# Cached attention on one core: PE's program for 24 of 32 batches written as a loop, with fixed slots for K and V

## The chip, the cores and the metric

The kernel runs on one core of a Trainium2 chip. The metric is the device time of one execution in microseconds; for the kernel before it is the median of three runs. A profiled execution is taken beside them.

## The reference

32 batches, 4 query positions each, 32 query heads and 4 K/V heads (8 query heads share one), 2048 cached positions, head size 128, all in bf16. It projects the queries, attends over the whole cache without a mask, and projects the result:

```python
q = (x @ wq).reshape(B, Sq, Hq, Dh).transpose(0, 2, 1, 3)     # x: [32, 4, 1024]
k = jnp.repeat(k_cache, rep, axis=1)                          # [32, 4, 2048, 128], rep = 8
v = jnp.repeat(v_cache, rep, axis=1)
scores = jnp.einsum("bhqd,bhkd->bhqk", q, k) * (Dh ** -0.5)
p = softmax(scores, axis=-1)
o = jnp.einsum("bhqk,bhkd->bhqd", p, v)
out = o.transpose(0, 2, 1, 3).reshape(B, Sq, Hq * Dh) @ wo    # wo: [4096, 1024]
```

K and V of one batch are 2 MB each, 128 MB over the 32 batches; wq and wo are 8 MB each.

## The kernel before, in words

**Data.** Every large load brings 2 MB (128 partitions of 16 KB) into one of seven slots of SBUF. The list `stream` gives the order: four pieces of wq, K of batches 0 and 1, and then, step by step, K of batch i+2 and V of batch i-2, at the end four slots' worth of wo. Load n goes to slot n % 7 and waits until the reader of load n-7 is done. SP issues all of them in this order, one queue, each behind the one before (L167 to L191), so a load that waits holds back all behind it.

**Work per batch.** PE does four things, in the order that the lists given to `pe_run` write out:
- `kt_fill`: K comes with positions on the partitions; 64 transposes against `ident`, in eight fills of eight, turn it over into three PSUM banks used as a ring (L250). DVE (five fills, L388) and ACT (fills 0, 1 and 7, L390) copy each fill to `KT_sb`, which has room for two batches. This is done two batches ahead.
- `qk`: 16 matmuls (four heads by four chunks of 512) write the scores of all 128 rows to `ps_s` (L262). DVE takes the row maximum (L445), ACT the exponential (L504), and DVE transposes the probabilities in blocks of 32 (L451); POOL (three groups of heads, L408) and ACT (one, L406) place them on the diagonal blocks of `PD_sb`, which has room for two batches.
- `pv`: 64 accumulating matmuls in four quarters against V (L281), two batches behind `qk`. DVE scales the result and masks it (L462).
- `o_tr`: four matmuls with `pick` transpose it (L310), DVE files it in `oT_sb` (L457).

Batch i on PE is: `qk` of i, fills 0 to 2 of batch i+2, the first two quarters of `pv` of i-2, fills 3 and 4, the other two quarters, fills 5 to 7, and `o_tr` of i-2. Batches 29 to 31 are interleaved by hand (`DRAIN` = 29), and then 64 matmuls project with wo (L362).

**Order and waits.** `Program` holds a list of operations per engine, written out in full for all 32 batches. Each engine has one semaphore that counts its named operations, each slot has one for its loads; `emit` puts a wait ahead of an operation for each semaphore whose value it needs and hasn't yet waited for. So PE's program is straight: 5064 matmuls and as many weight loads, one after the other.

The functions that the change touches, and what calls them:

Of the kernel before, what the change touches and what calls it, by code (L numbers as in the profile page):

```python
# [13 lines left out]
class Program:  # L14

    ENGINES = ("pe", "dve", "act", "pool", "sp")

    def __init__(self):
        self.ops = {e: [] for e in self.ENGINES}
        self.count = {e: 0 for e in self.ENGINES}
        self.event = {}

    def op(self, eng, fn, waits=(), name=None):
        if name is not None:
            assert name not in self.event, name  # L30
            self.count[eng] += 1
            self.event[name] = (eng, self.count[eng])
        self.ops[eng].append((tuple(waits), fn, name))

    def load(self, eng, fn, name, sem, value, waits=()):
        assert name not in self.event, name
        self.event[name] = (sem, value)
        self.ops[eng].append((tuple(waits), lambda e: fn(e).then_inc(self.sems[sem], 16), None))

    def emit(self, eng, handle):  # L40
        seen = {}
        for waits, fn, name in self.ops[eng]:
            need = {}
            for w in waits:
                s, n = self.event[w]
                need[s] = max(need.get(s, 0), n)
            for s, n in need.items():
                if seen.get(s, 0) < n:
                    handle.wait_ge(self.sems[s], n)
                    seen[s] = n  # L50
            ins = fn(handle)
            if name is not None:
                ins.then_inc(self.sems[eng], 1)


def bass_standalone__gqa_block_cached__sampling_kernel(
# [11 lines left out]
    REP = Hq // Hkv  # L68
# [6 lines left out]
    scale = float(Dh) ** -0.5  # L75
    NSLOT = 7
    SLOT = 8192
    NRING = 3
# [23 lines left out]
    with ExitStack() as es:  # L102
        sb = lambda name, shape, dt: es.enter_context(nc.sbuf_tensor(name, shape, dt))
        slots = sb("slots", [128, NSLOT, SLOT], BF16)
        KT_sb = sb("KT_sb", [128, 2, G, Sk], BF16)
        QT_sb = sb("QT_sb", [128, B, Hq, Sq], BF16)
        oT_sb = sb("oT_sb", [128, WE, WO_BLOCKS, NT], BF16)
# [23 lines left out]
        ps_oT = ring_f32[3][:, 256:384]  # L131
        late_o = [ring_f32[1][:, 0:128], ring_f32[3][:, 0:128]]
        late_oT = ring_f32[2][:, 0:128]

# [6 lines left out]

        pr.sems = {e: es.enter_context(nc.semaphore(f"s_{e}")) for e in Program.ENGINES}
        for n in ["x", "out", "v2"] + [f"slot{i}" for i in range(NSLOT)] + [f"wo{i}" for i in range(sum(map(len, WO_CUTS)))]:
            pr.sems[n] = es.enter_context(nc.semaphore(f"s_{n}"))


        stream = [("wq", i) for i in range(WQ_LOADS)] + [("k", b) for b in range(AHEAD)]
# [5 lines left out]
        stream += [("wo", i) for i in range(WO_LOADS)]  # L153
        slot_of = {l: n % NSLOT for n, l in enumerate(stream)}

        def freed(l):
            kind, i = l
            return {"wq": ("qproj", i), "k": ("kt", i, FILLS - 1), "v": ("pv", i, QUARTERS - 1)}[kind]

# [10 lines left out]
        n_wo = 0  # L170
        for n, l in enumerate(stream):
            kind, i = l
            waits = [freed(stream[n - NSLOT])] if n >= NSLOT else []
            s, v = f"slot{n % NSLOT}", 16 * (n // NSLOT + 1)
            if kind == "wq":
                pr.load("sp", fetch(slot(l), wq_v[:, i, :]), l, s, v, waits)
            elif kind in "kv":
                src = (k_cache if kind == "k" else v_cache)[i].rearrange("g (p t) d -> (g p) (t d)", t=NJ)
                if l == ("v", B - 1):
                    half = SLOT // 2  # L180
                    pr.load("sp", fetch(slot(l)[:, 0:half], src[:, 0:half]), l, s, v, waits)
                    pr.load("sp", fetch(slot(l)[:, half:], src[:, half:]), ("v2", i), "v2", 16, waits)
                else:
                    pr.load("sp", fetch(slot(l), src), l, s, v, waits)
            else:
                for k in range(i * BPL, (i + 1) * BPL):
                    for e0, e1 in WO_CUTS[k]:
                        at = (k - i * BPL) * WE * D
                        part = slot(l)[:, at + e0 * D:at + e1 * D]
                        pr.load("sp", fetch(part, wo_v[k][:, e0 * D:e1 * D]), ("wo", k, e0), f"wo{n_wo}", 16, waits)  # L190
                        n_wo += 1  # L191
        pr.op("sp", lambda e: e.dma_start(out_flat[:, :], out_sb).then_inc(pr.sems["out"], 16), ["out0", "out1"])
        pr.op("sp", lambda e: e.wait_ge(pr.sems["out"], 16))


        jobs = [("kt", b, f) for b in range(B) for f in range(FILLS)]
        job_index = {j: n for n, j in enumerate(jobs)}

        def consumer(b, f):
            return "act" if f in ACT_FILLS and (b, f) != (B - 1, FILLS - 1) else "dve"  # L200

        def ring_waits(job):
            n = job_index[job]
            if n < NRING:
                return [("q_evac", n)]
            return [("evac",) + jobs[n - NRING]]


        def last_in(r):
            return [job for n, job in enumerate(jobs) if n % NRING == r][-1]  # L210

# [24 lines left out]
        for a in range(WQ_LOADS):  # L236
            for j in range(NB):
                last = a == WQ_LOADS - 1
                name = ("q", j) if last else (("qproj", a) if j == NB - 1 else None)
                pr.op("pe", lambda e, a=a, j=j: pe_qproj(e, a, j), [("wq", a), "xT_evac"], name)  # L240
        pr.event[("qproj", WQ_LOADS - 1)] = pr.event[("q", NB - 1)]

        def kt_fill(b, f):
            job = ("kt", b, f)
            dst = ring_bf16[job_index[job] % NRING]

            def fn(e):
                for q in range(JPF):
                    j = f * JPF + q
                    ins = e.transpose(  # L250
                        dst[:, q * 128:(q + 1) * 128],
                        slot(("k", b))[:, j * Dh:(j + 1) * Dh],
                        ident[:, :],
                    )
                return ins

            pr.op("pe", fn, [("k", b)] + ring_waits(job), job)

        def qk(i, c):
            def fn(e):  # L260
                for g in range(G):
                    ins = e.matmul(  # L262
                        ps_s[32 * g:32 * (g + 1), c * 512:(c + 1) * 512],
                        lhsT=QT_sb[:, i, REP * g:REP * (g + 1), :],
                        rhs=KT_sb[:, i % 2, g, c * 512:(c + 1) * 512],
                        start=True,
                        stop=True,
                        tile_position=(0, 32 * g),
                    )
                return ins  # L270

            w = [("evac", "kt", i, f) for f in range(2 * c, 2 * c + 2)]
            if c == 0:
                w += [("q_evac", j) for j in range(NB)] if i == 0 else [("exp", i - 1)]
            pr.op("pe", fn, w, ("qk", i, c))

        def pv(b, quarter):
# [11 lines left out]

            w = [("v", b)] + [("place", b, g) for g in range(G)]  # L290
            if b == B - 1 and quarter >= QUARTERS // 2:
# [3 lines left out]
            elif b <= DRAIN - 2:  # L295
                w += [("o", b - 1), ("ot", b - 1)]
            elif b == DRAIN - 1:
                w += [("evac",) + last_in(1)]
            else:
                w += [("o", b - 2), ("ot", DRAIN - 2)]  # L300
            pr.op("pe", fn, w, ("pv", b, quarter))

        def o_tr(b):
            w = [("o", b), "pick"]
            if b >= DRAIN - 1:
                w += [("ot", b - 1), ("evac",) + last_in(2)]

# [28 lines left out]

        for i in range(DRAIN):
            steps = [("qk", i, ()), ("kt", i + AHEAD, (0, 1, 2))]
            if i >= LAG:
# [5 lines left out]
            if i >= LAG:  # L345
                steps.append(("ot", i - LAG, ()))
            pe_run(steps)
        pe_run([
            ("qk", B - 3, ()), ("kt", B - 1, (0, 1, 2, 3, 4, 5)),
# [32 lines left out]
        def evac(b, f):  # L382
            job = ("kt", b, f)
            src = ring_bf16[job_index[job] % NRING].rearrange("p (q g r) -> p g q r", g=G, r=32)
            dst = KT_sb[:, b % 2, :, f * JPF * 32:(f + 1) * JPF * 32].rearrange("p g (q r) -> p g q r", r=32)
# [73 lines left out]
        def dve_o(b):  # L459
# [4 lines left out]
                [("pv", b, QUARTERS - 1), ("rinv", b), "mask"] + ([("otr", b - 1)] if b > 0 else []), ("o", b))  # L464

        for i in range(DRAIN):
            dve_max(i)
            dve_fills(i + AHEAD, range(0, 5))
            dve_turn(i)
            if i >= LAG:  # L470
                dve_o(i - LAG)
# [51 lines left out]
        pr.op("act", lambda e: e.activation(out_sb[:, 512:1024], ps_s[:, 512:1024], ACT.Copy), [("oproj", 1)], "out1")  # L523

        block = es.enter_context(nc.Block())

# [49 lines left out]
```

## Time and profile before

| | |
|---|---|
| median of 3 runs | 370.23 us (370.18 to 370.35) |
| profiled execution | 370.08 us, of which the span is 368.3 us |
| granted TensorE clock | 0.995 |
| DMA | 152.24 MB, mean 413 GB/s over the span, 11711 packets |
| PE | busy 85% of the span; from 95 to 310 us 187.36 of 215 us |
| DVE, ACT, POOL | busy 69%, 65%, 50% |
| DMA share of the chain that ended last | 66% |

How to read it: a row of the page's groups or of a timeline has the line of the kernel, the engine, the operation with what it writes and reads, and times; in square brackets stands how long the engine was idle before, and what ended that. A row of a queue gives packets, MB and the share of the 16 DMA engines' span that the packets took. Queue q1 carries the kernel's loads and stores, q8 and q14 carry instructions. Rows that begin with "GB/s" cut their stretch of time into 40 equal slices. Time from issue to landing includes the time that a load stands behind others.

### The profile page before, as it was taken

The numbers are of one execution on the slowest core, as the hardware profiler recorded it, in microseconds if no ns is written. First come the engines' busy times: TensorE is split into PE (matmuls) and PEld (weight loads), VectorE is DVE, ScalarE is ACT, GpSimd is POOL, SyncE is SP. The second block draws the span as 40 slices with busy tenths as digits, with TensorE's granted clock in tenths as the row PEclk, the third lists the DMA queues.
The fourth block names the chain that finished last, engine by engine and source line by source line (L and its number), as shares of the span: only waits on it lengthen the run. The fifth ranks groups of instructions, "written<-read, shape, count | busy, mean of one in ns | idle before, by whom it ended". The sixth has DMA issues, their size and how long they took to land.

```text
span 368.3 us, 11026 instructions
## 1 busy us (share of the span) xinstructions
PE 312.9 (85%) x5062; PEld 271.5 (74%) x5064; DVE 254.3 (69%) x366; ACT 239.1 (65%) x197; POOL 186.0 (50%) x99
## 2 busy tenths in 40 slices
PE   0997867999988888878899888799888888899896
PEld 0896647888877777767788778697777777787842
DVE  0015877888877777778777777497778885799600
ACT  1016678888877778875777777678777775758200
POOL 9600066666655566665555555466666653547000
PEclk9999999999999999999999999899999999999999
DMA  8999999999999999999999999999999999999983
GB/s 319 432 429 427 432 424 425 421 425 427 425 423 427 424 425 429 425 425 430 426 425 424 424 425 427 425 425 425 425 427 423 424 424 429 431 421 415 422 352 121
DMA packets 11711, 152.24 MB, mean 413 GB/s; under 512 B 1296, under 2 KB 1296, under 8 KB 1936
## 3 DMA queue, kind: packets, MB, share of 16 engines
q1 hardware_dynamic: 11520, 151.26, 97.1%
q8 instruction: 40, 0.66, 0.7%
q10 hardware_dynamic: 144, 0.26, 0.2%
q14 instruction: 7, 0.06, 0.0%
HBM read 151.26 MB, written 0.26 MB: 411 GB/s over the span
## 4 chain that ended last, share of the span: by engine, by line
DMA 66%; PE 21%; ACT 9%; DVE 2%; issue 1%; SPq 0%
DMA slots<-in_v_cache_dram 52%; PE ps_o L281 10%; DMA slots<-in_k_cache_dram 7%; DMA slots<-in_wo_dram 7%; ACT KT_sb L390 5%; PE ps_a L250 3%; PE ps_b L250 3%; ACT P_sb L504 2%; ACT PD_sb L406 2%; PE ps_c L250 2%; DVE PC_sb L451 1%; PE ps_s L262 1%; PE ps_b L281 1%; PE ps_s L362 1%; DVE mx L445 1%
## 5 line engine op out<-in xcount | busy, mean ns | idle before, releaser
L408 POOL COPY PD_sb<-PC_sb 32x2048 bf16<-32x2048 bf16 x91 | 171.5, 1885 | 153.3 <-DVE PC_sb L451 144.9
L281 PE MATMUL ps_o<-slots,PD_sb 128*128 128x128 bf16 x1920 | 118.6, 220 | 29.8 <-DMA slots<-in_v_cache_dram 29.1
L281 PEld LDWEIGHTS ps_o<-slots,PD_sb 128*128 128x128 bf16 x1920 | 110.0, 99 | 34.1 <-DMA slots<-in_v_cache_dram 32.9
L406 ACT ACTIVATE PD_sb<-PC_sb 32x2048 bf16<-32x2048 bf16 x32 | 61.0, 1907 | 69.2 <-DVE PC_sb L451 69.2
L504 ACT ACTIVATE P_sb<-ps_s,negmx 128x2048 bf16<-128x2048 f32 x32 | 81.9, 2560 | 5.0 <-DVE negmx L446 4.3
L445 DVE TENSOR_REDUCE mx<-ps_s 128x1 f32<-128x2048 f32 x32 | 73.3, 2289 | 4.0 <-PE ps_s L262 3.2
L250 PE MATMUL ps_a<-ident,slots 128*128 128x128 bf16 x688 | 52.7, 219 | 3.4 <-DMA slots<-in_k_cache_dram 1.2
L250 PE MATMUL ps_c<-ident,slots 128*128 128x128 bf16 x680 | 52.4, 220 | 3.4 <-ACT KT_sb L390 2.1
L250 PE MATMUL ps_b<-ident,slots 128*128 128x128 bf16 x680 | 52.1, 219 | 2.1 <-ACT KT_sb L390 2.0
L388 DVE COPY KT_sb<-ps_c 128x1024 bf16<-128x1024 bf16 x54 | 36.8, 681 | 22.6 <-PE ps_c L250 22.4
L388 DVE COPY KT_sb<-ps_a 128x1024 bf16<-128x1024 bf16 x54 | 36.8, 681 | 18.7 <-PE ps_a L250 18.7
L388 DVE COPY KT_sb<-ps_b 128x1024 bf16<-128x1024 bf16 x53 | 36.1, 682 | 18.4 <-PE ps_b L250 18.3
L250 PEld LDWEIGHTS ps_a<-ident,slots 128*128 128x128 bf16 x688 | 41.0, 98 | 9.7 <-issue 5.2
L250 PEld LDWEIGHTS ps_c<-ident,slots 128*128 128x128 bf16 x680 | 40.9, 98 | 9.6 <-issue 5.2
L250 PEld LDWEIGHTS ps_b<-ident,slots 128*128 128x128 bf16 x680 | 40.4, 98 | 8.2 <-issue 4.2
L451 DVE STREAM_TRANSPOSE PC_sb<-P_sb 128x1024 uint32<-128x1024 uint32 x32 | 39.2, 1226 | 0.0
L390 ACT ACTIVATE KT_sb<-ps_a 128x1024 bf16<-128x1024 bf16 x32 | 32.8, 1025 | 3.5 <-PE ps_a L250 3.3
L390 ACT ACTIVATE KT_sb<-ps_b 128x1024 bf16<-128x1024 bf16 x32 | 32.8, 1024 | 2.9 <-PE ps_b L250 2.6
L262 PE MATMUL ps_s<-KT_sb,QT_sb 128*32 128x512 bf16 x512 | 33.5, 382 | 0.8 <-ACT P_sb L504 0.8
L390 ACT ACTIVATE KT_sb<-ps_c 128x1024 bf16<-128x1024 bf16 x31 | 31.7, 1024 | 0.2
L462 DVE SCALAR_TENSOR_TENSOR o_sb<-ps_o,rinv,mask 128x512 bf16<-128x512 f32 x30 | 21.4, 713 | 1.5 <-PE ps_o L281 1.5
L262 PEld LDWEIGHTS ps_s<-KT_sb,QT_sb 128*32 128x32 bf16 x512 | 10.7, 96 | 9.1 <-ACT P_sb L504 1.1
(46 smaller groups left out, 147.1 us busy)
## 6 DMA issues: line engine op xcount, KB each, us to landing
slots<-in_k_cache_dram SPq DMA_DIRECT2D x32, 2048.0 KB, 27.9
slots<-in_v_cache_dram SPq DMA_DIRECT2D x31, 2048.0 KB, 23.4
slots<-in_wq_dram SPq DMA_DIRECT2D x4, 2048.0 KB, 14.5
slots<-in_wo_dram SPq DMA_DIRECT2D x7, 1024.0 KB, 25.0
slots<-in_v_cache_dram SPq DMA_DIRECT2D x2, 1024.0 KB, 21.9
slots<-in_wo_dram SPq DMA_DIRECT2D x1, 512.0 KB, 25.4
slots<-in_wo_dram SPq DMA_DIRECT2D x2, 256.0 KB, 22.9
P_sb<-in_x_dram ACTq DMA_DIRECT2D x1, 256.0 KB, 8.1
```

Source lines behind the costliest of these rows:

```text
L250: ins = e.transpose(dst[:, q * 128:(q + 1) * 128], slot(("k", b))[:, j * Dh:(j + 1) * Dh], ident[:, :],)
L262: ins = e.matmul(ps_s[32 * g:32 * (g + 1), c * 512:(c + 1) * 512], lhsT=QT_sb[:, i, REP * g:REP * (g + 1), :], rhs=KT_sb[:, i % 2, g, c * ...
L281: ins = e.matmul(o_bank(b), lhsT=PD_sb[:, b % 2, j // 2, :, j % 2], rhs=v[:, j * Dh:(j + 1) * Dh], start=(j == 0), stop=(j == NJ - 1),)
L362: ins = e.matmul(ps_s[:, c * 512:(c + 1) * 512], lhsT=oT_sb[:, r, k, :], rhs=w[:, k % BPL, r, c * 512:(c + 1) * 512], start=(k == 0 and r ...
L388: pr.op("dve", lambda e: e.tensor_copy(dst, src), w, ("evac",) + job)
L390: pr.op("act", lambda e: e.activation(dst, src, ACT.Copy), w, ("evac",) + job)
L406: pr.op("act", lambda e: e.activation(dst, src, ACT.Copy), w, ("place", b, g))
L408: pr.op(eng, lambda e: e.tensor_copy(dst, src), w, ("place", b, g))
L445: pr.op("dve", lambda e: e.tensor_reduce(mx[:, i:i + 1], ps_s[:, :], AX.X, ALU.max), [("qk", i, 3)], ("max", i))
L451: pr.op("dve", lambda e: e.transpose(PC_flat[i % 2].bitcast(U32), P_sb.bitcast(U32)), [("exp", i)] + [("place", i - 2, g) for g in range(G ...
L462: pr.op("dve", lambda e: e.scalar_tensor_tensor(out=o_sb[:, :, :], in0=src, scalar=rinv[:, b:b + 1], in1=keep, op0=ALU.mult, op1=ALU.mult) ...
L504: pr.op("act", lambda e: e.activation(P_sb.rearrange("p (a r e) -> p a e r", r=32, e=2), ps_s[:, :].rearrange("p (a e r) -> p a e r", r=32 ...
```

## The change

**A loop on PE.** For batches 5 to 28 PE's program holds the operations of four batches once and runs them six times. `pe_loop` compares the six rounds, operation by operation: each event waited for must be the next in a row of six. It gives each such event of another engine a semaphore of its own that counts turns (`loop0`, `loop1`, ...), and drops waits on events that were waited for earlier in the same turn. `emit` writes the loop with a register `turn` and a register `landed` that rises by 16 for the DMA semaphores. Other engines' programs stay straight. To make the four batches identical in every turn:

- K of batch b (from 7) goes to slot b % 4, V of batch b (3 to 28) to slot 4 + b % 2. Earlier and later loads have slots by a table; the seventh slot takes one wq piece and the V of batches 0 and 29. The order of the loads is unchanged; what each waits for follows from the slot's last holder. The fourth wq piece counts as read when the whole Q projection is done.
- Fill f of a batch uses ring bank f % 3 whatever the batch, so a batch's first fill follows fill 6 of the batch before in its bank, the second fill 7, the third fill 5. The banks of the last batches' outputs are moved to match.
- Queries: DVE copies the 128x128 queries of batch i to one of two places in `QC_sb` (`dve_qc`, after the transposition of batch i-2 and ahead of `dve_o`), and `qk` reads them there for batches 5 to 28.
- `qk` no longer names the copies of its own K, and `pv` and `o_tr` name fewer events, since PE has already waited for these or for later ones of the same engine.

The diff, cut to its core:

```diff
+    def pe_loop(self, first, body, times):
+        self.loop = (first, body, times)
...
+                if same[0] in self.event:
+                    sem = self.event[same[0]][0]
+                    assert [self.event[e] for e in same] == [(sem, 16 * (n + 1)) for n in range(times)], same
+                    kept.append((sem, 16))
+                else:
+                    sem = f"loop{sum(map(len, self.body_waits)) + len(kept)}"
...
+                    kept.append((sem, 1))
...
+    def emit(self, eng, handle):
+        ops = self.ops[eng]
+        if eng != "pe":
+            self.straight(ops, eng, handle)
+            return
+        first, body, times = self.loop
+        self.straight(ops[:first], eng, handle)
+        landed = handle.alloc_register("landed")
+        handle.reg_mov(landed, 16)
+        with handle.Fori(1, times + 1) as turn:
+            for op, kept in zip(ops[first:first + body], self.body_waits):
+                for sem, step in kept:
+                    handle.wait_ge(self.sems[sem], turn if step == 1 else landed)
+                self.step(op, eng, handle)
+            handle.reg_add(landed, landed, 16)
+        self.straight(ops[first + body * times:], eng, handle)
...
+    BODY = 4
+    FIRST = 5
...
-        slot_of = {l: n % NSLOT for n, l in enumerate(stream)}
+        slot_of = {("wq", 0): 4, ("wq", 1): 5, ("wq", 2): 6, ("wq", 3): 3}
+        slot_of.update({("k", 0): 0, ("k", 1): 1, ("k", 2): 2, ("k", 3): 3, ("k", 4): 5, ("k", 5): 1, ("k", 6): 2})
+        slot_of.update({("v", 0): 6, ("v", 1): 0, ("v", 2): 4})
+        for b in range(FIRST + AHEAD, B):
+            slot_of["k", b] = b % 4
+        for b in range(FIRST - LAG, DRAIN):
+            slot_of["v", b] = 4 + b % 2
+        slot_of.update({("v", B - 3): 6, ("v", B - 2): 0, ("v", B - 1): 1})
+        slot_of.update({("wo", 0): 2, ("wo", 1): 3, ("wo", 2): 5, ("wo", 3): 4})
...
-            waits = [freed(stream[n - NSLOT])] if n >= NSLOT else []
-            s, v = f"slot{n % NSLOT}", 16 * (n // NSLOT + 1)
+            waits = [freed(held[slot_of[l]])] if slot_of[l] in held else []
+            held[slot_of[l]] = l
...
+        def bank(f):
+            return f % NRING
...
+        LAST_IN = {0: 6, 1: 7, 2: 5}
...
+        def ring_waits(b, f):
+            if f >= NRING:
+                return [("evac", "kt", b, f - NRING)]
+            return [("evac", "kt", b - 1, LAST_IN[f]) if b > 0 else ("q_evac", f)]
...
-                        lhsT=QT_sb[:, i, REP * g:REP * (g + 1), :],
+                        lhsT=(QC_sb[:, i % 2] if FIRST <= i < DRAIN else QT_sb[:, i])[:, REP * g:REP * (g + 1), :],
...
+        def dve_qc(i):
+            pr.op("dve", lambda e: e.tensor_copy(QC_sb[:, i % 2], QT_sb[:, i]),
+                  [("q_evac", j) for j in range(NB)] + ([("qk", i - 2, 3)] if i - 2 >= FIRST else []), ("qc", i))
...
+        loop_times = (DRAIN - FIRST) // BODY
+        assert (DRAIN - FIRST) % BODY == 0
+        pr.pe_loop(loop_first, (len(pr.ops["pe"]) - loop_first) // loop_times, loop_times)
```

## The prediction

> **What bounds the kernel now.** I read the page first: busy shares, then the queues.
>
> ```profile
> span 368.3 us, 11026 instructions
> ...
> PE 312.9 (85%) x5062; PEld 271.5 (74%) x5064; DVE 254.3 (69%) x366; ACT 239.1 (65%) x197; POOL 186.0 (50%) x99
> ...
> q1 hardware_dynamic: 11520, 151.26, 97.1%
> q8 instruction: 40, 0.66, 0.7%
> ...
> slots<-in_k_cache_dram SPq DMA_DIRECT2D x32, 2048.0 KB, 27.9
> slots<-in_v_cache_dram SPq DMA_DIRECT2D x31, 2048.0 KB, 23.4
> ```
>
> No engine is full, but the 16 DMA engines are: queue q1, the data, fills 97.1% of their span. The second queue is PE's own program: 40 packets and 0.66 MB, and 0.66 MB over PE's 5062 + 5064 instructions is 65 bytes each, so a packet of 16 KB is some 256 instructions. A load takes 23 to 28 us from issue to landing though 2 MB at 427 GB/s need 4.9 us: four or five loads are always queued.
>
> Next I asked what PE waits for. In the waits of 90 to 320 us and in PE's timeline:
>
> ```profile
> PEld ps_o L281 <- DMA slots<-in_v_cache_dram: 32.9, 22, 2.9
> ```
>
> ```profile
> 293.59 1.96 PE L281 MATMUL ps_o<-slots,PD_sb 128*128 128x128 bf16 x32 [1.18 <-DMA slots<-in_v_cache_dram]
> ...
> 304.96 1.96 PE L281 MATMUL ps_o<-slots,PD_sb 128*128 128x128 bf16 x32 [2.76 <-DMA slots<-in_v_cache_dram]
> ...
> 314.75 1.46 PE L281 MATMUL ps_o<-slots,PD_sb 128*128 128x128 bf16 x23 [1.18 <-DMA slots<-in_v_cache_dram]
> ```
>
> Each batch's first PV block starts when its V lands. The step is 9.79 us as a rule (two loads of 4.89) but now and then 11.37, as from 293.59 to 304.96. I wanted the reason, so I took the sixteen completion marks that the trace keeps for each load, one per DMA engine. For the first load they lie at 8.3 to 8.6 us; for the last W_O piece at 356.1 to 364.0. The earliest marks come every 4.893 us all the way, so some engines keep the full rate to the end. The latest fall behind them in five steps: 1.7 us after 23 us, 3.3 after 91, 4.7 after 160, 6.3 after 228, 8.0 after 292. Within a step the engines follow singly, each some 8.6 us after the last, and that is the spacing of the 40 instruction packets. So PE's packets go to eight engines in turn; each puts its engine back 1.6 us (8.0/5), and a load is complete only when the latest engine is. On two of the other engines the rarer fetches of DVE and ACT add up to 3.1 and about 1 us. The end of the kernel shows the same in the DMA answer for 350 to 368 us:
>
> ```profile
> GB/s 382 437 364 455 419 455 391 446 401 396 423 373 378 291 300 214 278 209 259 209 209 228 209 178 178 218 232 164 182 114 0 0 0 0 0 0 0 332 250 0
> ```
>
> From 356 us the rate is half: eight engines are through, eight have up to 8 us to go. Then 4.3 us of projection, copy and store to 368.3, and 1.8 us outside the span make 370.08, 0.15 below the median 370.23. In one line: the end is 356.1 + lag of the latest engine (7.9) + 4.3 + 1.8. What the change does to that lag decides.
>
> **The loop: how often PE's program is fetched.** A batch is 64 transposes, 16 QK, 64 PV and 4 output matmuls: 148, with weight loads 296 instructions. The loop writes four batches once for six turns, so 20 x 296 = 5920 of 10126 instructions disappear; 4206 stay, 16.4 packets. A body is 4 x 296 = 1184, with its waits about 1210: 4.7 packets.
> - If the body stays in PE's instruction memory, there are 16 packets that matter (in the kernel before, the fortieth came at 361.9 us, when its engine was nearly through). Over eight engines that is 2 each: lag 2 x 1.6 = 3.2, which is also what DVE's fetches leave on theirs, so no gain below that. 356.1 + 3.2 + 4.3 + 1.8 = 365.4. If a seventeenth falls before the end, 4.8 and 367.0.
> - If each turn fetches its body again, a turn costs 5 or 6 packets (a body of 4.7 that begins inside a block touches 5 or 6, and one is fetched ahead beyond the end). 11 outside the loop plus 36 to 40 make 47 to 51: 6 or 7 per engine, lag 9.6 to 11.2, total 371.8 to 373.4. If a block always goes to the same engine, one gets 7 or 8: up to 12.8 and 375.0.
>
> No row of this trace shows a jump back, so these two are the bounds, on both sides of zero. I take the first: the body is a small program, and eight engines taking turns for PE (DVE's three fetches all hit one engine) looks to me like eight places of 256 instructions, room for 4.7 blocks and one ahead. That is a weak reason, and I keep both ends.
>
> [...]
>
> **The jump itself.** If the target has to be fetched, PE stands still for it five times. Bounds: one packet, 1.07 us in the trace's packet records, to the 8.1 us that x takes from issue to landing; I take 3, a packet on top of the output's 2.0 us issue to landing. It hides in PE's waits for V: 1.2 us per batch, 4.7 per turn, and nothing after the last jump (about 275 us) is late by the end. Without that cover 5 x 3 = 15 us. If the target is there, a jump is nothing visible.
>
> **K in four slots, V in two.** Now a load waits for the load seven before it. After, V of batch b+2 waits for PV of batch b:
>
> ```profile
> 264.23 1.96 PE L281 MATMUL ps_o<-slots,PD_sb 128*128 128x128 bf16 x32 [1.19 <-DMA slots<-in_v_cache_dram]
> ...
> 266.92 1.95 PE L281 MATMUL ps_o<-slots,PD_sb 128*128 128x128 bf16 x32
> ```
>
> V lands at 264.2, its last PV ends at 268.9, so the next V is issued 4.9 us after the landing and the K behind it on SP at once (K's own slot came free four batches before). At that moment three loads, K, V and K, were ahead of it: 14.7 us. Margin for the latest engine: 14.7 - 4.9 - 2.0 (issue to landing of the small output store) = 7.8 us; an early engine has that less its lead, and where it runs dry it only loses lead. Towards the end, V of batch 28 has two loads ahead: margin 2.9. So nothing at the end moves, unless PE is later than that; then the excess is paid in full. V's issue to landing should fall to about 15 us, K's to 19. At the start K of batch 3 waits for the whole Q projection (28.5 us instead of 17.4), but K0 to K2 are in the queue until 37.7: nothing.
>
> **Waits, ring, copies.** The ring's first fill of a batch now waits for fill 6 of the batch before, its second for fill 7, which ACT copied out at 253.15 where PE began that fill at 252.47: 0.7 us later, with 0.6 to 1.2 us of waiting for V behind it; uncovered 24 x 0.7 = 17. Register waits: PE has 71 separate wait instructions of 51 ns now; five more per batch are 0.25 us, in the same cover. The 24 query copies on DVE: between 0.15 (128x1, L446) and 0.28 us (128x128 from PSUM, L457) each, after the transpose and ahead of the output scaling, for which PE's L310 waits; 24 x 0.28 = 6.7 us if uncovered, but DVE is 69% busy and PE's next wait is V. All zero in my sum; together they use most of a batch's 1.2 us, which is why the fourth case below has a chance.
>
> **The cases.** Smallest difference a measurement of this kernel can tell: about 0.2%, 0.7 us.
> 1. Body stays, 50%: 365.5, from 364.9 to 367.2. For it: the body is 4.7 blocks. Against: no row shows a block used twice.
> 2. Slower, body fetched every turn, 41%: 373.2, from 371.6 to 375.0. The place is the six turns' packets on PE's eight DMA engines; the price is 1.6 us for each packet above five on the latest engine. It decides from the point where PE keeps fewer blocks than the five or six of the body and the one ahead. The row that speaks for it is the 40 packets for 39.6 blocks, one new block at every crossing, which is what a memory without room for old blocks would show too.
> 3. No difference, 5%: 370.2. The loop runs, but the lag has another cause or the fetches stay as many and fall elsewhere. Against: steps and packets share spacing and count.
> 4. PE becomes the bound, 4%: stall, waits and ring use more than 4.7 us per turn. With a stall of 8.1 the excess is 3.4 in each of five jumps, on top of case 2: about 390.
>
> So faster 0.50, within 0.2% 0.05, slower 0.45. The predicted time is case 1's. The range reaches over case 2 to 374.0; left out are case 4, the upper fifth of case 2 and a little of case 1, about 0.15.
>
> **What would show it.** Right: the instruction queue q8 at 16 to 18 packets; none while the loop runs after its first turn; the sixteen marks of the last load within 3 to 5 us; PV steps of 9.8 us without one of 11.4; half rate at the end for 3 us instead of 8. Wrong: q8 at 45 or more, marks 10 us apart, an idle of PE above 1 us each fourth batch that ends in "issue"; then case 2. If V's issue to landing falls below 10 us or the DMA row shows gaps before 350 us, my margin for two V slots was wrong.

## The result and the profile after

The loop takes 365.65 us (365.61 to 365.71, four runs) against 370.21 us of the kernel before in the same session: ratio 0.9876, 95% interval 0.9859 to 0.9894. The forecast was 365.5. The profiled execution took 365.71 us, 363.9 of them the span, at a granted clock of 0.995.

From the page of the kernel after (busy time per engine; queues with packets, MB and share; loads with count, size and median time from issue to landing):

```profile
span 363.9 us, 11144 instructions
...
PE 313.3 (86%) x5062; PEld 271.5 (75%) x5064; DVE 256.2 (70%) x390; ACT 239.9 (66%) x197; POOL 186.0 (51%) x99
...
q1 hardware_dynamic: 11520, 151.26, 98.2%
q8 instruction: 16, 0.26, 0.3%
...
slots<-in_k_cache_dram SPq DMA_DIRECT2D x32, 2048.0 KB, 19.4
slots<-in_v_cache_dram SPq DMA_DIRECT2D x31, 2048.0 KB, 14.9
```

PE executes as many matmuls and weight loads as before, and q1 moves the same 151.26 MB. What has shrunk is q8: 16 packets instead of 40. In the trace's DMA records twelve of them lie between 21.0 and 118.4 us, four between 321.0 and 344.7, and none in the 203 us between, in which the second to sixth turns of the loop run (the first jump back is at 120.3 us, the sixth turn ends at 316.0).

What PE waits for from 90 to 320 us (engine, what it was about to do, what ended the wait: us in total, times, longest):

```profile
PEld ps_o L351 <- DMA slots<-in_v_cache_dram: 18.9, 21, 0.9
...
PE ps_b L317 <- ACT KT_sb L465: 6.8, 19, 0.4
...
PE ps_s L329 <- issue: 1.1, 5, 0.3
```

The first row had a longest wait of 2.9 us; it is 0.9 now. The other two rows are the two new costs on PE: the ring's second fill (6.8/19 = 0.36 us) and the five jumps back (1.1/5 = 0.22 us). In PE's timeline, a jump and two first PV blocks (start, time, what, idle time before it and its end):

```profile
120.84 1.05 PE L329 MATMUL ps_s<-KT_sb,QC_sb 128*32 128x512 bf16 x16 [0.25 <-issue]
...
300.49 1.96 PE L351 MATMUL ps_o<-slots,PD_sb 128*128 128x128 bf16 x32 [0.73 <-DMA slots<-in_v_cache_dram]
...
310.27 1.96 PE L351 MATMUL ps_o<-slots,PD_sb 128*128 128x128 bf16 x32 [0.72 <-DMA slots<-in_v_cache_dram]
```

The step is 310.27 - 300.49 = 9.78 us; in this stretch the kernel before had one of 11.37. At the end, the DMA rate from 350 to 364 us in 40 slices of 0.35 us:

```profile
GB/s 445 421 398 398 445 374 445 468 421 421 363 398 433 392 415 421 410 380 258 269 257 199 228 234 211 94 0 0 0 0 0 0 0 0 0 310 386 53 0 0
```

The reduced rate lasts from about 356.3 to 359.1, 2.8 us; in the row of the kernel before it lasts from about 356.3 to 363.5, 7.2 us. The sixteen completion marks of the last load lie at 356.75 to 359.53, where they were at 356.1 to 364.0. So the last piece of data is complete 4.47 us earlier, and the time falls by 4.56.

### The profile page after: what moved, and what is told of

The parts are those of the page before. It is cut to its first block, busy times and chain, and to the rows that moved or that the text cites. A ratio compares the mean times of both kernels' runs of the same rounds, so it can differ in the third digit from the quotient of the medians.

```text
span 363.9 us, 11144 instructions
## 1 busy us (share of the span) xinstructions
PE 313.3 (86%) x5062; PEld 271.5 (75%) x5064; DVE 256.2 (70%) x390; ACT 239.9 (66%) x197; POOL 186.0 (51%) x99
## 3 DMA queue, kind: packets, MB, share of 16 engines
q1 hardware_dynamic: 11520, 151.26, 98.2%
HBM read 151.26 MB, written 0.26 MB: 416 GB/s over the span
## 4 chain that ended last, share of the span: by engine, by line
DMA 59%; PE 29%; ACT 6%; DVE 3%; issue 1%; SPq 0%
DMA slots<-in_v_cache_dram 45%; PE ps_o L351 17%; DMA slots<-in_k_cache_dram 7%; DMA slots<-in_wo_dram 7%; PE ps_b L317 4%; ACT KT_sb L465 4%; PE ps_a L317 3%; PE ps_s L329 2%; PE ps_c L317 1%; DVE KT_sb L463 1%; ACT PD_sb L481 1%; PE ps_c L351 1%; PE ps_s L437 1%; DVE PC_sb L526 1%; ACT P_sb L585 1%
## 5 line engine op out<-in xcount | busy, mean ns | idle before, releaser
L463 DVE COPY KT_sb<-ps_a 128x1024 bf16<-128x1024 bf16 x64 | 43.8, 685 | 48.8 <-PE ps_a L317 48.7
L317 PE MATMUL ps_b<-ident,slots 128*128 128x128 bf16 x768 | 59.8, 221 | 11.6 <-ACT KT_sb L465 11.2
L465 ACT ACTIVATE KT_sb<-ps_b 128x1024 bf16<-128x1024 bf16 x63 | 64.6, 1025 | 5.1 <-PE ps_b L317 4.4
L317 PE MATMUL ps_a<-ident,slots 128*128 128x128 bf16 x768 | 59.1, 220 | 5.4 <-DVE KT_sb L463 3.6
L317 PEld LDWEIGHTS ps_a<-ident,slots 128*128 128x128 bf16 x768 | 45.9, 98 | 19.2 <-issue 15.8
L463 DVE COPY KT_sb<-ps_c 128x1024 bf16<-128x1024 bf16 x64 | 43.5, 680 | 6.1 <-PE ps_c L317 6.1
L317 PE MATMUL ps_c<-ident,slots 128*128 128x128 bf16 x512 | 39.6, 221 | 0.0
L317 PEld LDWEIGHTS ps_c<-ident,slots 128*128 128x128 bf16 x512 | 31.7, 99 | 0.2 <-DVE KT_sb L463 0.2
L329 PE MATMUL ps_s<-KT_sb,QC_sb 128*32 128x512 bf16 x384 | 25.1, 381 | 1.1 <-issue 1.1
L463 DVE COPY KT_sb<-ps_b 128x1024 bf16<-128x1024 bf16 x33 | 22.5, 681 | 0.6 <-PE ps_b L317 0.6
L437 PE MATMUL ps_s<-slots,oT_sb 128*128 128x512 bf16 x62 | 13.9, 379 | 1.0 <-DVE oT_sb L532 0.6
## 6 DMA issues: line engine op xcount, KB each, us to landing
slots<-in_k_cache_dram SPq DMA_DIRECT2D x32, 2048.0 KB, 19.4
slots<-in_v_cache_dram SPq DMA_DIRECT2D x31, 2048.0 KB, 14.9
```

What stands on the lines that cost most here:

```text
L317: ins = e.transpose(dst[:, q * 128:(q + 1) * 128], slot(("k", b))[:, j * Dh:(j + 1) * Dh], ident[:, :],)
L329: ins = e.matmul(ps_s[32 * g:32 * (g + 1), c * 512:(c + 1) * 512], lhsT=(QC_sb[:, i % 2] if FIRST <= i < DRAIN else QT_sb[:, i])[:, REP * ...
L437: ins = e.matmul(ps_s[:, c * 512:(c + 1) * 512], lhsT=oT_sb[:, r, k, :], rhs=w[:, k % BPL, r, c * 512:(c + 1) * 512], start=(k == 0 and r ...
L463: pr.op("dve", lambda e: e.tensor_copy(dst, src), w, ("evac",) + job)
L465: pr.op("act", lambda e: e.activation(dst, src, ACT.Copy), w, ("evac",) + job)
```

## The experiments

A "mark" is one of the sixteen completions that the trace keeps per load, one per DMA engine; "last mark" is the latest of the last W_O piece. Neither a mark nor a packet says which engine it belongs to: that is inferred from how the marks of a load lie. Times are medians, or single executions where the table says so, with the ratio to the kernel before on the same chip; on the chips of these runs that kernel took 370.10 to 370.25. The runs together:

| kernel | PE's packets | last mark, us | time, us | ratio (95%) |
|---|---|---|---|---|
| before | 40 | 364.0 | 370.21 | |
| after | 16 | 359.53 | 365.65 | 0.9876 (0.9859 to 0.9894) |
| e1: PE's program straight | 40 | 363.96 | 370.33 | 1.0002 (0.9993 to 1.0012) |
| e3: loop for half the batches | 30 | 362.46 | 368.78 | 0.996 (0.9945 to 0.9974) |
| e4: 20 rows of 16 KB | 16 | 375.06 | 381.47 | 1.0305 (1.0288 to 1.0322) |
| e5: the same rows in two loads | 16 | 364.47 | 370.64 | 1.0016 (1.0006 to 1.0025) |
| e10: the same bytes in one even load | 16 | 360.49 | 366.55 | 0.9906 (0.989 to 0.9923) |
| e6: body of 5.95 blocks | 18 | 379.70 | 387.16 | one execution |
| e7: body of 6.95 blocks | 64 | 466.21 | 473.87 | one execution |
| e2: body of eight batches | 43 | 366.67 | 372.46 | 1.0051 (1.0035 to 1.0068) |
| e8: the same with a hint | 42 | 365.46 | 373.49 | 1.0092 (1.0061 to 1.0123) |
| e11: V of batch 28 in the seventh slot | 16 | 359.59 | 365.72 | 0.9879 (0.9863 to 0.9896) |

The theory: PE's packets put eight DMA engines back, one at a time, and the kernel ends with the latest engine ("lag"). Rivals: the gain comes from what was rearranged for the loop, that is slots, ring, query copies and waits ("schedule"); or from the 0.39 MB that is no longer moved ("bytes").

**e1: everything but the loop.** Slots, ring banks, query copies and events are those of the kernel after; PE's program is written out.

```diff
-        if eng != "pe":
+        if True:
             self.straight(ops, eng, handle)
             return
```

> The changed kernel with PE's program written out straight again; slots, ring banks, query copies and the semaphores are the changed kernel's. Lag theory (the end is set by the DMA engine that PE's instruction packets put back most, 1.6 us each, eight engines in turn): 40 packets on q8, last load's marks 7 to 8 us apart or less only because early engines run dry, 370.2 us within 0.7. Schedule theory (fixed slots, ring banks and copies brought the gain): 365.7 with 40 packets. Bytes theory (0.4 MB less to fetch, shared by all 16 engines, 24 x 1.07 / 16 = 1.6 us): 367.3.

Measured 370.33 us. From its page, and from its DMA answer for 350 to 368 us (slices of 0.45 us):

```profile
span 368.6 us, 11124 instructions
...
q8 instruction: 40, 0.66, 0.7%
```

```profile
GB/s 400 455 419 401 455 382 400 437 437 401 473 400 401 437 401 419 382 419 437 419 382 446 373 382 410 364 246 209 200 118 0 0 0 0 0 0 0 100 378 105
```

With 40 packets the whole gain is gone, so the schedule theory falls. The rate row has a surprise: the long half-rate stretch is absent. The marks of the last load are only 1.9 us apart (362.05 to 363.96), yet the last one is where it was. With two slots for V the early engines had run dry at V of batch 28 (first mark at 327.3 where the full rate gives about 321.4) and lost their lead. The spread at the end is therefore no safe sign of the lag; the last mark is.

**e3: half the loop.** Batches 5 to 16 straight, 17 to 28 as three turns.

```diff
     FIRST = 5
+    LOOP_FIRST = 17
...
-        loop_times = (DRAIN - FIRST) // BODY
+        loop_times = (DRAIN - LOOP_FIRST) // BODY
```

> The loop only for batches 17 to 28 (three turns), batches 5 to 16 straight; everything else as changed. Lag theory: 16 + 12 x 303 / 256 = 30 packets, 3 or 4 per engine, lag 6.0 to 6.4, so 2.8 to 3.6 above 365.65: 368.4 to 369.3. Bytes theory: 14 packets x 1.07 / 16 = 0.9 above: 366.6. Schedule theory: 365.7.

Measured 368.78 us. Its page:

```profile
q8 instruction: 30, 0.49, 0.5%
```

Thirty packets over eight engines are at most four on one: 356.1 + 4 x 1.6 = 362.5, and the last mark is at 362.46. Lag theory met; bytes and schedule, which wanted 366.6 and 365.7, not.

**e4: delay without instructions.** To see whether a packet delays only its own engine, 20 rows of 16 KB, each a load to one partition and each in one packet, are put behind V of batches 5 to 24, into the free seventh slot. 327,680 bytes in all. V of batch 29, the next in that slot, waits for the last row, which landed at 306.3 us, before that load's turn came.

```diff
+            if l == ("v", B - 3):
+                waits.append(("row", LAST_ROW))
...
+                if kind == "v" and 5 <= i < 25:
+                    r = i - 5
+                    dst_row = slots[r:r + 1, 6, :]
+                    src_row = src[r:r + 1, :]
+                    pr.load("sp", fetch(dst_row, src_row), ("row", r), "row", 16 * (r + 1), [("pv", 0, QUARTERS - 1)])
```

> The changed kernel with 20 extra rows of K, 16 KB each and one packet each, loaded by SP behind the V of batches 5 to 24 into the seventh slot and never read: 0.33 MB, about what the loop saves in instruction bytes. Lag theory: if all rows go to one engine, it falls behind by 20 x 0.61 = 12.2 us on top of its own 0 to 3; the last marks stand 9 to 13 us later: 375 to 378. Bytes theory: 0.33 MB at 427 GB/s = 0.8 us: 366.4.

Measured 381.47 us, beyond the forecast. The rows left one completion each, where a load of 2 MB leaves sixteen (q1 has 11560 packets instead of 11520: twenty of 16 KB and twenty completions), so each ran on one engine, and by the marks it was the same for all: in the load whose first mark is at 199.23 us fifteen marks lie within 3.4 us, the sixteenth 8.6 behind the first. The last mark moved from 359.53 to 375.06, 0.78 us per row. I had taken 0.61, which is 16 KB at one engine's sixteenth of 427 GB/s. In the middle of the run a batch took 10.86 us by its last marks (235.3, 246.1, 256.9, 267.9) instead of 9.79, so 1.07 per row. The first rows only used up that engine's lead: the last marks are those of the kernel after until 153.6 us and fall behind from the next load on. At 1.07 each, 14 to 15 of the twenty rows make the 15.53 us, an estimate. The kind of effect is shown, the size of one row's delay was forecast too low. From 200 to 320 us (busy time with counts for PE, PEld, DVE, ACT, POOL; then clock, DMA share, rate):

```profile
200.00:320.00 120.00, 101.82 (x1650) 90.64 (x1648) 85.60 (x136) 81.30 (x66) 62.21 (x33) 0.96 0.97 399
```

Here one late engine held back all: V's slot comes free only when its latest part has been used, so the others ran dry, and the rate fell from the 428 GB/s of the kernel after (95 to 310 us) to 399.

**e5: the same rows in two loads.** Rows 0 to 15 beside V of batch 5, 16 to 19 beside V of batch 15.

```diff
+                if kind == "v" and i in (5, 15):
+                    r = i - 5
+                    lo, hi = ((0, 16), (16, 20))[r // 10]
+                    dst_row = slots[lo:hi, 6, :]
+                    src_row = src[lo:hi, :]
+                    pr.load("sp", fetch(dst_row, src_row), ("row", r), "row", 16 * (r // 10 + 1), [("pv", 0, QUARTERS - 1)])
```

> The same 20 extra rows of 16 KB as in the run with twenty single rows, but in two loads, 16 rows beside the V of batch 5 and 4 beside that of batch 15; never read. Lag theory: a load of 16 rows puts one on each engine, so every engine falls back by 0.6 to 1.1 us once and four engines twice: 0.6 to 2.1 above 365.65, 366.3 to 367.8. If the cost of the single rows was that of issuing many loads and not of the one engine, it falls in proportion, to 2/20 of 15.8 us: 367.2. Bytes theory: 366.4.

A miss: 370.64 us. The load of 16 rows did spread over the engines, but the marks show every engine 3.0 us late after it, and the small load took another 0.4 to 1. A further 0.95 of the 4.94 us at the last mark appears at 276.0 us, in the first load after a packet of q14 (272.1); no run follows that up. The rate from 98 to 112 us (slices of 0.35 us):

```profile
GB/s 468 374 421 328 515 468 421 468 375 281 187 281 94 234 421 234 281 187 140 140 140 375 234 515 234 304 468 281 421 421 421 421 515 421 375 375 468 468 375 421
```

For about 6 us, from 101 to 107, it lies mostly at 94 to 304. The 262 KB to 16 partitions put every engine back by 3.0 us, where 2 MB to all 128 take 4.9. No run here varied the partitions alone, so the reason for the 3.0 us is not shown, and e5 could not separate bytes from places.

**e10: the same bytes, evenly.** One load of 2560 bytes to each of 128 partitions, 327,680 bytes, beside V of batch 5.

```diff
+                if kind == "v" and 5 <= i < 6:
+                    r = i - 5
+                    dst_row = slots[:, 6, 0:1280]
+                    src_row = src[:, 0:1280]
+                    pr.load("sp", fetch(dst_row, src_row), ("row", r), "row", 16 * (r + 1), [("pv", 0, QUARTERS - 1)])
```

> The 0.33 MB of the twenty single rows once more, never read, now as one load over all 128 partitions (2560 bytes each) beside the V of batch 5, so that it is shared by engines and partitions as the kernel's own loads are. Lag theory: each of the 16 engines falls back by 20 KB at 27 GB/s = 0.8 us, none more than the others: 366.4. If the 15.8 us of the single rows, or the 5.0 of the two loads, came from the bytes or from the loads as such, it costs 5 or more: 370.6.

Measured 366.55 us, 0.90 above the kernel after; 0.33 MB at 427 GB/s are 0.77. The same bytes cost 0.9 us in one load on all engines and 15.8 in twenty loads on one. PE's 24 missing packets are 0.39 MB, 0.92 us if spread evenly; the change gained 4.56. So the number of bytes is not the cause, their place is.

**e6 and e7: how much PE keeps.** The fills of batches 7 to 30, those in the loop, repeat 5 or 9 of their transposes (the first result is overwritten by the same values). The forecasts put the body at about 1550 and 1806 instructions; the trace's records of one turn count 1523 and 1779, which is 5.95 and 6.95 blocks of 256 (1203, or 4.7, in the kernel after). PE becomes the bound (in e6 busy for 160.00 of the 160 us from 140 to 300), so here packets and idle times decide, not the total. The diff is that of e6; e7 has `range(9)`.

```diff
-                for q in range(JPF):
+                again = range(5) if FIRST + AHEAD <= b < DRAIN + AHEAD else ()
+                for q in [r % JPF for r in again] + list(range(JPF)):
```

> The changed kernel with 5 transposes in each fill of the loop written twice (same result), so that the body is 320 instructions longer, about 1550 or 6.1 blocks of 256. Only the packets of the instruction queue are read; PE becomes the bound by 40 x 0.056 us a batch and the time rises to 390 or more. If PE keeps eight blocks (7 or 8 with the one ahead): 17 or 18 packets. If it keeps fewer than seven: about 16 + 5 x 7 = 50. If the loop's blocks are kept whatever their number up to nine: 18.

> As the run before with 9 transposes more per fill: 576 instructions longer, about 1806 or 7.1 blocks, which touch eight and one ahead is a ninth. Only the packets are read; the time rises past 410. If PE keeps eight blocks: the turns fetch again, 16 + 5 x 8 or more = 50 to 60 packets; if it keeps nine or more: 19.

The packets of e6, then those of e7, each from its page:

```profile
q8 instruction: 18, 0.29, 0.3%
```

```profile
q8 instruction: 64, 1.05, 0.9%
```

And e7's waits from 60 to 330 us:

```profile
PE ps_s L330 <- issue: 26.0, 4, 6.6
```

5.95 blocks are kept, with no packet between 128.7 and 348.9 us; 6.95 blocks are fetched again in each turn, and each jump in this window leaves PE idle for about 6.5 us. The 64 packets are more than the 50 to 60 of the forecast: 45 above the 19 of a kept body, nine for each of the five jumps. The limit lies between the two bodies; where between them, no run shows. e6's time, 387.16 us, is a little under the 390 of its forecast. e7 is 86.7 us slower than e6: 24 x 8 x 4 = 768 more transposes at 56 ns (a fill of eight every 0.45 us) are 43, and five jumps are 33. Most of the remaining 11 goes with the lower clock, 0.957 against 0.995: in the clock records of e7 a stretch of 6.8 us at half the clock begins inside each of the five pauses, and 19.1 us of these stretches lie behind the pauses, where half speed loses 9.6, an estimate.

**e2: a jump whose target is gone.** The body is emitted twice per turn: three turns of eight batches, two jumps. The forecast took 9.6 blocks for the body; the records of a turn count 2403 instructions, 9.4.

```diff
+COPIES = 2
...
-        with handle.Fori(1, times + 1) as turn:
+        turn = handle.alloc_register("turn")
+        handle.reg_mov(turn, 1)
+        with handle.Fori(0, times // COPIES):
+            for copy in range(COPIES):
...
+                handle.reg_add(turn, turn, 1)
```

> The loop with its four-batch body written twice: three turns of eight batches, about 2450 instructions or 9.6 blocks of 256, same semaphores, same work. If PE keeps about eight blocks, each turn fetches its 10 to 12 blocks again: 40 to 47 packets on q8, 5 or 6 per engine, lag 8 to 9.6, 370.4 to 372; two jumps of about 3 us each hidden by PE's waits for V. If PE keeps a dozen blocks or more: 16 + 5 = 21 packets, 3 per engine on most, lag 4.4 to 4.8, 367.2. Schedule theory: 365.7 in both.

Measured 372.46 us. Its page, the two jumps in PE's timeline, and two windows after the second (columns as in e4):

```profile
q8 instruction: 43, 0.70, 0.8%
```

```profile
165.86 1.47 PE L337 MATMUL ps_s<-KT_sb,QC_sb 128*32 128x512 bf16 x12 [6.08 <-issue]
...
247.18 1.90 PE L337 MATMUL ps_s<-KT_sb,QC_sb 128*32 128x512 bf16 x16 [6.20 <-issue]
```

```profile
248.00:254.00 6.00, 6.00 (x79) 5.16 (x72) 3.14 (x3) 3.89 (x3) 0.00 (x0) 0.69 1.00 423
254.00:260.00 6.00, 5.64 (x100) 4.80 (x98) 5.88 (x10) 4.04 (x5) 3.32 (x2) 1.00 0.78 289
```

Each jump back to a block that was gone cost 6.1 to 6.2 us of PE here, where the forecast had 3, hidden, and the second cost more behind it: the granted clock is 0.69 in the first window (one half up to 251.7 us by the clock records), so `qk` takes 1.90 us instead of 1.05. PV ends late, the next V is issued at 256.3 us instead of 249.3 in e1, and in the second window the DMA engines are busy for only 0.78 of the time. Against e1, with 40 packets, the last mark is 2.7 us later (366.67 against 363.96). Load by load the last marks stand 0.1 us later than e1's behind the first jump (184.42 against 184.31) and 1.4 behind the second (265.52 against 264.10). The other 1.4 come with a step at 341.85 (339.08 in e1) that looks like one more packet on the latest engine: 43 packets over eight engines put six on some. So about half of the loss is the second jump and half the packets.

**e8: the same with a hint.** The loop is written with `hint_back_edge`, an instruction at the head of each turn that names the coming jump.

```diff
-        with handle.Fori(0, times // COPIES):
+        with handle.bass.Fori(0, times // COPIES, engines=[handle.engine], hint_back_edge=True):
```

> The eight-batch body again, with an instruction at the head of each turn that names the branch at its end, so that the branch's target can be fetched ahead. If the 2.1 us that the eight-batch body costs above the straight program come from the two jumps (6.1 and 6.2 us of PE idle, PE's clock down after them), they go: PE idle before the scores of batches 13 and 21 under 0.5 us, 43 to 45 packets, 370.3 to 371. If they come from its three packets more: 372.4 as before.

Measured 373.49 us (372.21 to 374.53), not better. PE's timeline:

```profile
161.71 1.05 PE L337 MATMUL ps_s<-KT_sb,QC_sb 128*32 128x512 bf16 x16 [1.90 <-issue]
...
243.11 1.05 PE L337 MATMUL ps_s<-KT_sb,QC_sb 128*32 128x512 bf16 x16 [1.77 <-issue]
...
328.49 1.91 PE L359 MATMUL ps_o<-slots,PD_sb 128*128 128x128 bf16 x31 [2.66 <-issue]
```

With the hint a jump leaves PE idle for 1.77 to 1.90 us instead of 6.08 to 6.20, where the forecast had under 0.5, with `qk` at its usual 1.05. The step behind the second jump is gone (264.37 against e1's 264.10), and the last mark comes 1.2 us earlier than in e2. It is still 1.5 later than e1's: with 42 packets a step of 1.3 remains, at 350.28 (349.00 in e1), and six packets on the latest engine would give 356.1 + 6 x 1.6 = 365.7 where 365.46 was measured. So jumps and packets each made about half of what the marks lost in e2. The time fits neither figure of the forecast: a new stall of 2.66 us appears behind the loop's end, and 5.4 us pass from the last mark to the end of the span instead of 4.4. There PE is late: at the end it works through the projection without a wait, where in the kernel after it had waited for the last pieces. The two rows, e8's first:

```profile
360.67 7.07 PE L445 MATMUL ps_s<-slots,oT_sb 128*128 128x512 bf16 x31
```

```profile
357.11 3.63 PE L437 MATMUL ps_s<-slots,oT_sb 128*128 128x512 bf16 x15 [0.27 <-DMA slots<-in_wo_dram]
```

Why the stall behind the loop appears, and why these runs spread over 2.3 us, stays open.

**e11: the early engines' dry spell.** V of batch 28 goes to the seventh slot, V of 29 to slot 4, the last piece of wo to slot 6.

```diff
-        slot_of.update({("v", B - 3): 6, ("v", B - 2): 0, ("v", B - 1): 1})
-        slot_of.update({("wo", 0): 2, ("wo", 1): 3, ("wo", 2): 5, ("wo", 3): 4})
+        slot_of.update({("v", B - 4): 6, ("v", B - 3): 4, ("v", B - 2): 0, ("v", B - 1): 1})
+        slot_of.update({("wo", 0): 2, ("wo", 1): 3, ("wo", 2): 5, ("wo", 3): 6})
```

> The changed kernel with V of batch 28 in the free seventh slot (V of 29 takes the slot that 28 had), so that it is issued at once and no early engine runs dry at 316 to 322 us. Lag theory: the first mark of the last load moves from 356.7 back to 356.1, the last mark stays at 359.5, and the time stays at 365.65 within 0.2. If the early engines' dry spell costs time: 0.6 less, 365.0.

Measured 365.72 us against 365.65. The first mark of the last load is back at 356.10, the last stays at 359.59: the early engines that ran dry in the kernel after lost lead (first mark at 356.75) and no time.

## Why the prediction was right, point by point

- **The sum.** Predicted 356.1 + 3.2 + 4.3 + 1.8. Measured: the last mark at 359.53, which is a lag of 3.4 counted from 356.1; 4.4 to the end of the span; 1.8 outside it. e11, with the first mark at 356.10, shows that this is the right zero; in the kernel after the first mark itself had moved to 356.75. That is also why its sixteen marks lie only 2.8 us apart where 3 to 5 were forecast.
- **The lag and its price.** Shown: 40 packets (five on an engine) end at 364.0, 30 (four) at 362.46, 16 (two) at 359.53; a step of 1.6 us per packet fits all three within 0.3. Which engine a packet falls on is inferred from the marks. That a delay on one engine costs the whole kernel is shown by e4 against e10 (381.47 and 366.55 us with the same 327,680 bytes).
- **Whether the body stays.** Right, with luck: nothing in the trace of the kernel before could tell it, the reason was called weak, and at 50 against 41 the choice was almost even. The eight places of 256 instructions in it were my estimate, and no run shows that number: 5.95 blocks are kept (e6), 6.95 are not (e7), and no body between them was run. The body has the 4.7 blocks that were forecast, less than either. In the other case the sum had a slip: six turns of 6 or 7 packets are 36 to 42, not 36 to 40; the lag of six or seven packets stays the same.
- **The jump.** "Nothing visible" was 0.22 us on average, in the cover of the waits for V. For a target that is gone I took 3 us between bounds of 1.07 and 8.1; e2 has 6.1 to 6.2. That term was half of what was measured, and it left out the clock: behind the second stall of e2 it was 0.69 from 248 to 254 us. Neither counted here, since the target was there.
- **Slots.** V took 14.9 us from issue to landing (predicted about 15), K 19.4 (19). The thin margin at V of batch 28 was real: early engines ran dry there, at no cost.
- **Ring and copies.** The second fill waits 0.36 us where I had taken 0.7. A query copy takes 0.152 us, the lower end of 0.15 to 0.28. PE has 121 separate wait instructions instead of 71, two more per batch in place of five. All this shrinks PE's wait for V, 1.2 us per batch before and 0.73 now; that wait did not vanish, so they cost nothing, and the fourth case stayed away. e1 has them all and ends with the kernel before.
- **The rivals.** The body fetched each turn is no idle fear: e7 shows it at 6.95 blocks. "No difference from another cause" is refuted by e1 and e3.

## What to carry to other kernels

When the DMA engines are the bound (q1 filled 97.1% of their span here), ask for the latest engine rather than the mean rate. Here, as the marks are read, each 16 KB packet of PE's program put one engine back by 1.6 us, and PE waited for the last of a load's sixteen marks: in the kernel before one V had its marks at 277.39 to 283.75 us, and its first PV block began at 283.80. The loop paid here with a body of 4.7 blocks of 256 instructions, which was fetched once, and with waits that could be written the same in every turn; a body of 5.95 blocks (e6) was not fetched again either, one of 6.95 (e7) was, in each turn. With 9.4 blocks (e2) it saved no fetches (43 packets against the 40 of e1), each of its two jumps left PE idle for 6.1 to 6.2 us, and it took 2.1 us more than the program written out (e1).

## What the runs showed of the hardware that I had not expected

- Behind the second jump of e2, 6.20 us without work to 247.18 us, PE's granted clock was 0.69 from 248 to 254 us. In the clock records a stretch of 6.8 us at half the clock begins 3.2 to 4.1 us into each of the seven pauses of over 6 us at a jump (two in e2, five in e7); shorter stretches at half the clock also occur without such a pause (in the kernel before one of 3.4 us at 235.2 us).
- The same 327,680 bytes cost 15.8 us as twenty single rows on one DMA engine, 5.0 as two loads of 16 and 4 rows, and 0.9 as one load over all 128 partitions (e4, e5, e10, each against the kernel after).
- With a hint ahead of the jump PE was still idle for 1.8 to 1.9 us at each (6.1 to 6.2 without it), and a stall of 2.66 us followed behind the loop (e8).
